# Two wide row loads put at passes 10 and 13, and the sums of three weight tiles kept from the first mixing for the second

## The chip, the cores and the metric

The kernel runs on one core of one Trainium2 chip. The metric is the device time of one execution in microseconds (us); the median of several runs counts. A profiled execution has a time of its own and a span, which is the time from its first instruction to its last. Matrix products run on TensorE (PE in the profile's rows; PEld is its loading of weights), elementwise work on VectorE (DVE) and ScalarE (ACT), and DMAs are issued by SyncE (SP) and GpSimd (POOL).

## The reference

Four layers on an x of 2048 rows by 512 columns in float32. Layers 0 and 2 are a Fourier mixing, layers 1 and 3 a gated feed-forward network:

```python
def _A_ref(x, dft_seq_re, dft_seq_im, dft_hid_re, dft_hid_im):
    a = jnp.einsum("bsd,ed->bse", x, dft_hid_re)
    b = jnp.einsum("bsd,ed->bse", x, dft_hid_im)
    return jnp.einsum("ts,bse->bte", dft_seq_re, a) - jnp.einsum("ts,bse->bte", dft_seq_im, b)

def _B_ref(x, w_gate, w_up, w_down):          # 512 -> 1792 -> 512
    return (_gelu(x @ w_gate) * (x @ w_up)) @ w_down

x = A_x
x = x + _A_ref(_layernorm(x), ...)
x = x + _B_ref(_layernorm(x), ...)
x = x + _A_ref(_layernorm(x), ...)
x = x + _B_ref(_layernorm(x), ...)
```

## The kernel before

Every float32 product is made of three: each operand is split into a high part of reduced precision and the rest, and high by high, high by rest and rest by high are summed (`mm3`, lines 211 to 215). A split (`split`, lines 154 to 158) is a copy on ScalarE (L156) and a subtraction on VectorE (L158). Tiles of 128 x 512 live in 98 slots of on-chip memory, which are taken and given back in order; the two wide tiles, `xwide` and `wide`, hold 512 rows of x each and are lent out as eight more slots while they are not used for x.

**The products take seven multiplications in place of eight** (Strassen's way, in a form with few additions). So operands are cut in four quarters A11, A12, A21, A22, and sums S1 to S4 of them are needed. In a mixing (layers 0 and 2) the sequence matrix is worked through in four blocks of 512 output rows. For each block the stages are A11, A12, S2 (which holds the products with S2, S1 and S3), S4, and the products with the hidden matrix. With `FORE` at 4, all four blocks run A11 first, then all four run A12, then block 0 goes on with S2. For each k of 8 in S2, `make_s2` takes the loaded tiles a21, a22 and a11 and makes three sums of them on VectorE (one addition, L196, and two subtractions, L189); `make_s4` makes the fourth from a12. The matrix is the same in layers 0 and 2. For two tiles of the last block the sums are made ahead, in layer 1 (`summed_ahead`), stored in `wss`, and loaded by the second mixing.

**The feed-forward layers** run in two windows of 1024 rows (w = 0, 1). A window has 14 passes (`up`) over the gate and up matrices, with products of the down matrix beside them (`beside`), and then the remaining products of the down matrix (the `late` list). With all seven pairs of the hidden blocks done in the seven-product form (`SEVEN` is 7: layer 1 in both windows and layer 3 in its first), the window's result is added to two wide tiles of x (`turned_into`) which `load_turned(0)` and `load_turned(1)` fill with four DMAs of 256 KB each (L1508, through `moved`), and `rows_done` stores them (L1515). `beside` calls `load_turned(0)` in the fourteenth pass; another call follows behind the passes, and `load_turned(1)` comes a third of the way through `late`.

**Other work in the queues.** In layer 1's second window row tiles of x are loaded (L241) for the statistics that the next mixing's normalisation needs (`terms_ahead`, `norm_terms`, L614 to L619 on ScalarE), and `seed` (L207) copies a bank of sums on ScalarE so that TensorE can go on adding to it.

**What sets the order.** Each engine and each DMA queue runs its own instructions in a fixed order. That order is made when the kernel is built: a planner goes through the program with its own durations, and an engine that is free takes the next instruction whose inputs it thinks ready, so a load can be pulled far ahead of its place in the program. `tc.issue_after(i)` is how the program holds this back: an instruction traced under it stands behind i in its engine's order, without a wait of its own. `stream["last"]` is the latest load of the stream of matrix tiles (`load_next`, L333), which runs a bounded number of items ahead of the products.

Of the kernel before, what the change touches and what calls it, by code (L numbers as in the profile page):

```python
# [9 lines left out]
F32 = mybir.dt.float32  # L10
# [4 lines left out]
P = 128  # L15
# [5 lines left out]
NB = S // TB  # L21
# [8 lines left out]
LAG = 6  # L30
NEAR = 3, 2, 6
EARLY = 2
EARLY_FROM, EARLY_EACH = 8,2
PACE = 9
SKEW = 2, 1
# [10 lines left out]
LATER = 3  # L46
LET = 5
SUMMED = 2
DOWN_RUNS = ((0,0,0,0),(4,4,4,0),(4,4,4,0),2)


@with_exitstack
def fnet_geglu(ctx: ExitStack, tc: tile.TileContext, x_in, ws, wh, wgu, wdn, wdc, whc, out):
# [32 lines left out]
    nc = tc.nc  # L86
# [80 lines left out]
    def split_slot(src):  # L167
        hi, lo = sb.get(F32R), sb.get(F32R)
        split(src, hi, lo)
        return hi, lo  # L170
# [129 lines left out]
    whs = {(m, c): dram.tile([P, 1024], F32, name=f"wh{m}_{c}") for m in range(2) for c in range(ND)}  # L300
    wds = {f: dram.tile([P, 1024], F32, name=f"wd{f}") for f in range(NF)}
    wdd = {k: dram.tile([P, 7 * 512], F32, name=f"wc{k}") for k in range(NF // 2)}
    wss = {k: [dram.tile([P, 512], F32, name=f"ws{k}_{i}") for i in range(4)] for k in range(SUMMED)}
    whd = {k: dram.tile([P, 7 * 512], F32, name=f"wq{k}") for k in range(ND)}
    pieces = (("A11", "A12"), ("S2", "S3"), ("S1", "A22"), ("S4",))

# [54 lines left out]
    def plain(v):  # L361
        p = split_slot(v)
        sb.put(v)
        return p
# [20 lines left out]
            return split_slot(v)  # L385
        return run

    def make_s2(k):
        def run(a21, a22, *a11):
            a11 = a11[0] if a11 else held.pop(k)  # L390
            plus(a22, a21, a22)
            minus(a21, a11, a21)
            minus(a11, a22, a11)
            s1s[k], s2s[k], s3s[k] = a22, a11, a21
            return split_slot(a11)
        return run

# [3 lines left out]
    def make_s3(k):  # L401
        return lambda: plain(s3s.pop(k))

    def make_s4(k):
        def run(a12):
            v = s2s.pop(k)
            minus(a12, a12, v)
            sb.put(v)
            return plain(a12)
        return run  # L410

# [74 lines left out]
    NP = NF // 2  # L486
# [16 lines left out]
    def mix_items(layer):  # L503
        def raw(make, *tiles):
            items.append((F32, tiles, make, None))

        for b, what in plan(layer):
            tiles = [[ws[(b * 2 + m) * NS + k] for k in range(NS)] for m in range(2)]
            (a11, a12), (a21, a22) = ((r[:NK], r[NK:]) for r in tiles)
            hold = b >= FORE[layer]  # L510
            if what == "A11":
                for k in range(NK):
                    raw(as_is if bare(layer, b, what, k) else make_a11(k) if hold else plain, a11[k])
            elif what == "A12":
                for k in range(NK):
                    raw(plain, a12[k])
            elif what == "S2":
                for i, k in skewed(3):
                    if layer and b == NB - 1 and k < SUMMED:
                        raw(plain, wss[k][i])  # L520
                    elif i == 0:
                        raw(make_s2(k), a21[k], a22[k], *(() if hold else (a11[k],)))
                    else:
                        raw(make_s1(k) if i == 1 else make_s3(k))
            elif what == "S4":
                for i, k in skewed(2):
                    if layer and b == NB - 1 and k < SUMMED and i == 0:
                        raw(plain, wss[k][3])
                    elif i == 0:
                        raw(make_s4(k), a12[k])  # L530
                    else:
                        raw(plain, a22[k])
            elif b in PAIRED.get(layer, ()):
                items.extend(pair_items(what))
            else:
                for m, c in what:
                    if layer == 0 and b == 0:
                        items.append((F32, (wh[m * ND + c],), make_hid_first(m, c), (m, c)))
                    else:
                        items.append((F32R, halves(whs[m, c]), make_hid(m, c), (m, c)))  # L540
# [666 lines left out]
    def summed_ahead(k):  # L1207
        t = []

        def load():  # L1210
            for m, i in ((1, k), (1, NK + k), (0, k), (0, NK + k)):
                t.append(sb.get())
                with tc.issue_after(stream["last"].ins):
                    nc.sync.dma_start(t[-1], ws[((NB - 1) * 2 + m) * NS + i])

        def sums():
            before, in_order[0] = in_order[0], True
            a21, a22, a11, a12 = t
            plus(a22, a21, a22)
            minus(a21, a11, a21)  # L1220
            minus(a11, a22, a11)
            minus(a12, a12, a11)
            for to, v in zip(wss[k], (a11, a22, a21, a12)):
                nc.gpsimd.dma_start(to, v)
            sb.put(*t)
            in_order[0] = before

        return load, sums
# [29 lines left out]
    def geglu(w, layer):  # L1258
# [77 lines left out]
        def beside_next(n, down):  # L1336
            beside_mix(n)
            next(down, None)

        def up(n):  # L1340
            if n + 3 in making:
                making[n + 3][0]()
            if n + 2 in making:
                queue.extend(making[n + 2][1])
            if n > 2 or w:
                for _ in range(DOWN_RUNS[3]):
                    run = down_making.pop(0) if down_making else None
                    if run:
                        run()
            product(n, chain[n], "S2", "T2", False, True)  # L1350
            u[n] = copied(chain[n])
            down = beside(n)
            beside_next(n, down)
            side[n] = ps8.get()
            product(n, side[n], "S1", "T1", True, True)
            w4[n] = copied(side[n])
            beside_next(n, down)
            first(n + 1)
            beside_mix(n)
            product(n, chain[n], "S3", "T3", False, True)  # L1360
            v = w4.pop(n)
            plus(v, v, chain[n])
            finished(n, 1, 1, v)
            sb.put(v)
            beside_next(n, down)
            product(n, side[n], "S4", "B22", False, True)
            v = u.pop(n)
            plus(v, v, side[n])
            ps8.put(side.pop(n))
            finished(n, 0, 1, v)  # L1370
            sb.put(v)
            beside_next(n, down)
            second(n + 1)
            if pairs == NP:
                for name, k in down_order(layer, w)[1][:max(0, n - EARLY_FROM) * EARLY_EACH]:
                    if k in h4:
                        prepared(name, k)
            product(n, chain[n], "A22", "T4", False, True)
            ps = chain.pop(n)
            if n % 2 == 0:  # L1380
                v = copied(ps)
                finished(n, 1, 0, v)
                sb.put(v)
            else:
                finished(n, 1, 0, ps)
            ps8.put(ps)
            beside_next(n, down)
            for _ in down:
                pass
# [111 lines left out]
        def outside(at, part):  # L1501
            return begun[part] if at == layer + 1 and pairs < NP else xs[at, w * 2 + part]

        def load_turned(part):
            assert part or not sb.out("x")
            pool = tpool if part else upool
            xturned[part] = pool.tile([P, NT * D], F32, name="wide" if part else "xwide")
            moved(xturned[part], outside(layer, part), lambda v, rows: nc.sync.dma_start(v, rows))  # L1508

        def turned_rows(part, c, src):  # L1510
            turned_into(xturned[part], c, src)
# [89 lines left out]
                slow.pop(0)()  # L1601
        if plain_down:
            load_rows(0)
        elif pairs == NP:
            load_turned(0)
        if w == 0:
            queue.extend([None] * 9 + others[len(ahead_of_all):ND] + ([] if ahead_of_all else [None] * 4) + others[ND:])
# [20 lines left out]
        else:  # L1628
# [3 lines left out]
            for i, (name, k) in enumerate(late):  # L1632
                if name == "S4" and pairs < NP:
                    break
                if pairs < NP and name == "S1" and k > 1:
                    prepared("S4", k - 2)
                for more in late[i:i + EARLY + 1]:
                    prepared(*more)
                for _ in down_product(name, k):
                    pass  # L1640
                if i == len(late) - HOLD:
                    late_end.append(newest["PE"])
                if not before_mix or i % 3 == 0:
                    step()
                if before_mix and i == len(late) // 2:
                    stream["more"] = MORE
                if i == len(late) // 3:
                    load_turned(1)
                    if w == 0:
                        queue[:2 * len(ahead)] = [run for pair in zip(ahead, queue) for run in pair] + queue[len(ahead):2 * len(ahead)]  # L1650
                while w == 0 and len(queue) > 2 * (len(late) - 1 - i):
                    step()
# [123 lines left out]
```

## Time and profile before

| | |
|---|---|
| three runs | 1596.91, 1599.49, 1601.11 us; median 1599.49 |
| profiled execution | 1599.44 us, span 1597.5 us |
| DMA | 431.74 MB, mean 270 GB/s |
| HBM | 344.46 MB read, 85.72 MB written |
| granted TensorE clock | full throughout |

A row of a group or of a time-ordered view gives a start and a length in us (or count, busy time and mean), the engine, the line of the kernel, the operation, what it writes and reads (buffer numbers left out), and in square brackets how long the engine idled before it and who ended the wait. "SPq" is the SP queue's issuing. Rows of a stretch give its two ends, its length, the busy time of each engine with its count of instructions, the granted clock, the DMA engines' busy share and GB/s; asked for one engine or line, they show that alone. Matmuls overlap, so a busy TensorE is best judged by the distance between starts.

### The profile page before, as it was taken

What the parts mean: (1) busy time and instruction counts of PE and PEld (TensorE: products, weight loads), DVE (VectorE), ACT (ScalarE), POOL (GpSimd) and SP (SyncE); (2) the same over time, 40 slices, a digit from 0 to 9 for tenths busy, and PEclk for the clock granted to TensorE, in tenths of its full rate; (3) what the DMA queues carried; (4) which work ended last, traced back from release to release, by engine and by line L of the source; (5) the groups of instructions that cost most, each with busy time, mean ns of one, the idle gap of its engine ahead of it and who ended that gap; (6) DMA issues with size and microseconds to landing.
All of it is one profiled execution on the core that took longest, in us unless ns stands there. A gap on an engine that the chain in (4) does not pass through costs nothing.

```text
span 1597.5 us, 22834 instructions
## 1 busy us (share of the span) xinstructions
PE 1589.7 (100%) x6984; PEld 1310.1 (82%) x6984; DVE 1176.7 (74%) x2042; ACT 890.4 (56%) x1731; POOL 293.6 (18%) x493
## 2 busy tenths in 40 slices
PE   9999999999999999999999999999999999999999
PEld 6888888888888888788888888888888888888887
DVE  8997878888689794665879867777895557844573
ACT  8955465754767653566648545556553565333460
POOL 4112121351457101330031000001301000000000
PEclk9999999999999999999999999999999999999999
DMA  9878888996998999997895876878978968895445
GB/s 363 290 264 295 305 307 280 356 309 202 316 363 315 278 323 294 350 361 238 290 299 187 272 242 213 271 247 249 257 257 277 273 213 256 296 295 173 132 145 158
DMA packets 249433, 431.74 MB, mean 270 GB/s; under 512 B 29344, under 2 KB 74656, under 8 KB 248288
## 3 DMA queue, kind: packets, MB, share of 16 engines
q1 hardware_dynamic: 220464, 340.36, 67.3%
q0 software_dynamic: 26160, 87.84, 15.3%
q10 hardware_dynamic: 2688, 2.10, 0.5%
q8 instruction: 55, 0.90, 0.2%
q14 instruction: 66, 0.54, 0.1%
HBM read 344.46 MB, written 85.72 MB: 269 GB/s over the span
## 4 chain that ended last, share of the span: by engine, by line
PE 90%; DMA 3%; issue 3%; ACT 2%; DVE 1%; POOL 1%; SPq 0%; POOLq 0%; ACTq 0%; DVEq 0%
PE p L214 30%; PE p L213 30%; PE p L215 30%; DMA s<-t 1%; ACT s L156 1%; DVE s L158 1%; PE p L999 1%; DMA xwide<-x 1%; DMA s<-x 1%; DMA s<-ws 0%; POOL rstd L617 0%; PE p L1682 0%; ACT s L200 0%; ACT p L207 0%; DVE s L189 0%
## 5 line engine op out<-in xcount | busy, mean ns | idle before, releaser
L214 PE MATMUL p<-s,s 128*128 128x512 f32 x2312 | 897.7, 389 | 0.8 <-DVE s L158 0.8
L215 PE MATMUL p<-s,s 128*128 128x512 f32 x2312 | 892.3, 389 | 0.0
L213 PE MATMUL p<-s,s 128*128 128x512 f32 x2312 | 858.2, 389 | 1.6 <-ACT p L207 1.5
L156 ACT ACTIVATE s<-s 128x512 fp32r<-128x512 f32 (+1 forms) x859 | 483.1, 608 | 266.1 <-DVE s L189 66.9
L158 DVE TENSOR_TENSOR s<-s,s 128x512 fp32r<-128x512 f32 (+1 forms) x859 | 540.1, 663 | 111.9 <-ACT s L156 94.8
L213 PEld LDWEIGHTS p<-s,s 128*128 128x128 f32 x2312 | 433.8, 188 | 93.6 <-ACT p L207 2.6
L214 PEld LDWEIGHTS p<-s,s 128*128 128x128 f32 x2312 | 433.9, 188 | 92.1 <-DVE s L158 2.3
L215 PEld LDWEIGHTS p<-s,s 128*128 128x128 f32 x2312 | 433.9, 188 | 90.4
L193 DVE TENSOR_TENSOR s<-s,p 128x512 f32<-128x512 f32 x199 | 134.7, 683 | 163.2 <-PE p L215 136.6
L189 DVE TENSOR_TENSOR s<-s,s 128x512 f32<-128x512 f32 (+1 forms) x415 | 245.1, 612 | 4.7 <-DMA s<-ws 2.2
L200 ACT ACTIVATE s<-p 128x512 f32<-128x512 f32 x232 | 134.4, 593 | 112.6 <-PE p L215 108.5
L1253 ACT ACTIVATE s<-s 128x512 f32<-128x512 f32 x84 | 52.8, 628 | 46.4 <-DVE s L193 46.1
L617 POOL TENSOR_SCALAR rstd<-rstd 128x1 f32<-128x1 f32 x40 | 23.2, 580 | 239.3 <-ACT s L616 231.5
L1253 ACT ACTIVATE s<-p 128x512 f32<-128x512 f32 x28 | 16.7, 596 | 83.2 <-PE p L215 83.2
L319 POOL DMA_DIRECT2D wb<-s x84 | 46.2, 552 | 91.2 <-ACT s L156 68.9
L640 ACT ACTIVATE s<-s,shift,rstd 128x512 f32<-128x512 f32 x59 | 47.6, 812 | 16.9 <-DVE shift L607 9.7
L1269 DVE TENSOR_TENSOR s<-s,p 128x512 f32<-128x512 f32 x56 | 38.3, 684 | 24.7 <-PE p L215 24.7
L158 DVE TENSOR_TENSOR s<-xwide,s 128x512 fp32r<-128x512 f32 (+1 forms) x49 | 32.8, 679 | 25.2 <-ACT s L156 25.2
L196 DVE TENSOR_TENSOR s<-s,s 128x512 f32<-128x512 f32 (+1 forms) x73 | 44.2, 613 | 6.8 <-DMA s<-ws 3.8
L207 ACT ACTIVATE p<-p 128x512 f32<-128x512 f32 x56 | 32.6, 584 | 24.2 <-PE p L215 23.9
L729 DVE STREAM_TRANSPOSE wide<-s 128x512 f32<-128x512 f32 x31 | 21.9, 708 | 25.8 <-ACT s L640 21.8
L1190 POOL DMA_DIRECT2D wc<-s x42 | 30.6, 730 | 54.0 <-ACT s L156 36.3
(104 smaller groups left out, 621.8 us busy)
## 6 DMA issues: line engine op xcount, KB each, us to landing
s<-ws SPq DMA_DIRECT2D x406, 256.0 KB, 5.0
s<-wb SPq DMA_DIRECT2D x294, 256.0 KB, 5.2
s<-wc SPq DMA_DIRECT2D x182, 256.0 KB, 4.6
wb<-s POOLq DMA_DIRECT2D x98, 256.0 KB, 5.2
s<-wh SPq DMA_DIRECT2D x84, 256.0 KB, 5.3
s<-x SPq DMA_DIRECT2D x53, 256.0 KB, 5.3
wc<-s POOLq DMA_DIRECT2D x49, 256.0 KB, 5.3
xwide<-ws SPq DMA_DIRECT2D x36, 256.0 KB, 4.9
```

The source lines that it names most:

```text
L156: newest["ACT"] = nc.scalar.activation(hi, src, AF.Copy)
L158: newest["DVE"] = nc.vector.tensor_tensor(lo, src, f32(hi), op=ALU.subtract)
L189: nc.vector.tensor_tensor(out, a, b, op=ALU.subtract)
L193: bank_read["DVE"] = nc.vector.tensor_tensor(out, a, b, op=ALU.add)
L196: nc.vector.tensor_tensor(out, a, b, op=ALU.add)
L200: bank_read["ACT"] = nc.scalar.activation(v, src, AF.Copy)
L213: nc.tensor.matmul(ps, ah, bh, start=start, stop=False, skip_group_check=True)
L214: nc.tensor.matmul(ps, ah, bl, start=False, stop=False, skip_group_check=True)
L215: newest["PE"] = nc.tensor.matmul(ps, al, bh, start=False, stop=stop, skip_group_check=True)
L319: nc.gpsimd.dma_start(a, f32(t))
L640: nc.scalar.activation(z, x, AF.Identity, bias=shift, scale=rstd)
L1253: nc.scalar.activation(t, g, AF.Gelu_apprx_tanh)
```

## The change

Two things are changed. In layer 1's second window `load_turned(0)` is called in the tenth pass and `load_turned(1)` in the thirteenth; in that window their DMAs are put behind the latest load of the matrix stream. The calls behind the passes and in `late` are left out where the tile is there already; the call in `beside` stays as it was. And in the first mixing's block 0 the four sums of tiles k = 0, 1, 2 are stored to memory by GpSimd's queue as they are made; the second mixing's block 0 loads them in place of the tiles and the sums.

```diff
+TURNED = 9, 12
+KEPT = ((0, 0), (0, 1), (0, 2))
...
-    wss = {k: [dram.tile([P, 512], F32, name=f"ws{k}_{i}") for i in range(4)] for k in range(SUMMED)}
+    wss = {
+        (b, k): [dram.tile([P, 512], F32, name=f"ws{b}_{k}_{i}") for i in range(4)]
+        for b, k in [*KEPT, *((NB - 1, k) for k in range(SUMMED))]
+    }
...
+    def sums_kept(layer, at, sums):
+        if layer == 0 and at in KEPT:
+            for i, v in sums.items():
+                nc.gpsimd.dma_start(wss[at][i], v)
+
-    def make_s2(k):
+    def make_s2(layer, b, k):
         def run(a21, a22, *a11):
             a11 = a11[0] if a11 else held.pop(k)
             plus(a22, a21, a22)
             minus(a21, a11, a21)
             minus(a11, a22, a11)
             s1s[k], s2s[k], s3s[k] = a22, a11, a21
+            sums_kept(layer, (b, k), {0: a11, 1: a22, 2: a21})
             return split_slot(a11)
...
-    def make_s4(k):
+    def make_s4(layer, b, k):
         def run(a12):
             v = s2s.pop(k)
             minus(a12, a12, v)
             sb.put(v)
+            sums_kept(layer, (b, k), {3: a12})
             return plain(a12)
...
-                    if layer and b == NB - 1 and k < SUMMED:
-                        raw(plain, wss[k][i])
+                    if layer and (b, k) in wss:
+                        raw(plain, wss[b, k][i])
...
-                    if layer and b == NB - 1 and k < SUMMED and i == 0:
-                        raw(plain, wss[k][3])
+                    if layer and (b, k) in wss and i == 0:
+                        raw(plain, wss[b, k][3])
...
             beside_next(n, down)
+            if (layer, w) == (1, 1) and n in TURNED:
+                load_turned(TURNED.index(n))
             side[n] = ps8.get()
...
-            moved(xturned[part], outside(layer, part), lambda v, rows: nc.sync.dma_start(v, rows))
+            with tc.issue_after(stream["last"].ins) if (layer, w) == (1, 1) else ExitStack():
+                moved(xturned[part], outside(layer, part), lambda v, rows: nc.sync.dma_start(v, rows))
...
-        elif pairs == NP:
+        elif pairs == NP and not xturned:
             load_turned(0)
...
                 if i == len(late) // 3:
-                    load_turned(1)
+                    if 1 not in xturned:
+                        load_turned(1)
```

More of the change, by code (lines that the diff above doesn't have):

```diff
@@ L518, in mix_items @@
                 for i, k in skewed(3):
-                    if layer and b == NB - 1 and k < SUMMED:
-                        raw(plain, wss[k][i])
+                    if layer and (b, k) in wss:
+                        raw(plain, wss[b, k][i])
                     elif i == 0:
-                        raw(make_s2(k), a21[k], a22[k], *(() if hold else (a11[k],)))
+                        raw(make_s2(layer, b, k), a21[k], a22[k], *(() if hold else (a11[k],)))
                     else:
@@ L526, in mix_items @@
                 for i, k in skewed(2):
-                    if layer and b == NB - 1 and k < SUMMED and i == 0:
-                        raw(plain, wss[k][3])
+                    if layer and (b, k) in wss and i == 0:
+                        raw(plain, wss[b, k][3])
                     elif i == 0:
-                        raw(make_s4(k), a12[k])
+                        raw(make_s4(layer, b, k), a12[k])
                     else:
@@ L1222, in sums @@
             minus(a12, a12, a11)
-            for to, v in zip(wss[k], (a11, a22, a21, a12)):
+            for to, v in zip(wss[NB - 1, k], (a11, a22, a21, a12)):
                 nc.gpsimd.dma_start(to, v)
```

## The prediction

> **What bounds the kernel now.** I read the page first (engine totals and the chain), then the list of who waited for whom on TensorE, then the time-ordered views around each stall, and last the stretches into which the change moves work.
>
> ```profile
> span 1597.5 us, 22834 instructions
> PE 1589.7 (100%) x6984; PEld 1310.1 (82%) x6984; DVE 1176.7 (74%) x2042; ACT 890.4 (56%) x1731; POOL 293.6 (18%) x493
> ...
> PE p L213 <- ACT p L207: 1.5, 2, 1.3
> PE p L1682 <- POOL ident masks.py:199: 1.4, 1, 1.4
> PE p L214 <- DVE s L158: 0.8, 1, 0.8
> ```
>
> The first two lines are the page, the last three are all the waits of TensorE: 3.7 us in the whole span, of which 1.4 us lie in the warm-up. TensorE sets the time, the change touches no matmul (x6984 stays), so it can only win back stalls or add new ones. Two stalls matter, and each part of the change stands beside one of them. The first, in order of time on TensorE, on ScalarE and on the SP queue:
>
> ```profile
> 642.73 0.39 PE L214 MATMUL p<-s,s 128*128 128x512 f32 x1
> 642.95 0.39 PE L215 MATMUL p<-s,s 128*128 128x512 f32 x1
> 644.67 0.50 PE L213 MATMUL p<-s,s 128*128 128x512 f32 x1 [1.33 <-ACT p L207]
> 645.01 0.40 PE L214 MATMUL p<-s,s 128*128 128x512 f32 x1
> ...
> 643.41 0.63 ACT L614 ACTIVATE s<-s 128x512 f32<-128x512 f32 x1 [3.63 <-DMA s<-x]
> ...
> 644.04 0.58 ACT L207 ACTIVATE p<-p 128x512 f32<-128x512 f32 x1
> ...
> 615.99 2.78 SPq L1508 DMA_DIRECT2D wide<-x  x4
> 618.88 3.08 SPq L1243 DMA_DIRECT2D s<-wb  x2
> 622.13 4.01 SPq L1508 DMA_DIRECT2D xwide<-x  x4
> ...
> 635.76 3.29 SPq L1508 DMA_DIRECT2D xwide<-x  x4
> ...
> 634.60 8.79 DMA s<-x
> ...
> s<-x SPq DMA_DIRECT2D x53, 256.0 KB, 5.3
> ```
>
> Matmuls start 0.22 to 0.23 us apart; from 642.95 to 644.67 it is 1.72, so 1.49 is lost, and the next start comes 0.34 later, another 0.11: 1.60 us. TensorE waits for the seed of a bank (L207). That seed is ready to run but stands on ScalarE behind L614, the statistics of a row tile for the next mixing, which idled 3.63 us for its load. That load took 8.79 us (last but one line, from the chain) against a median of 5.3 (last line, the page). Eight DMAs of wide tiles stand just ahead of it on SP, and four more just behind it: all twelve belong to this very window (layer 1, second half), though the program asks for them 120 us later or more. They were pulled ahead as soon as the tiles were free.
>
> The second stall:
>
> ```profile
> 889.64 1.07 PE L213 MATMUL p<-s,s 128*128 128x512 f32 x4
> 891.55 0.50 PE L214 MATMUL p<-s,s 128*128 128x512 f32 x1 [0.84 <-DVE s L158]
> 891.88 0.39 PE L215 MATMUL p<-s,s 128*128 128x512 f32 x1
> ...
> 891.12 1.07 POOL L291 DMA_DIRECT2D m_sum<-s  x2 [6.12 <-ACT s L200]
> ...
> 872.00:891.50 19.50, 19.50 (x34) 1.00 0.87 292
> 872.00:891.50 19.50, 6.43 (x11) 1.00 0.87 292
> 872.00:891.50 19.50, 3.44 (x5) 1.00 0.87 292
> ...
> 876.95 4.91 DMA s<-ws
> ...
> 884.18 0.69 DVE L196 TENSOR_TENSOR s<-wide,s 128x512 f32<-128x512 f32 x1
> ```
>
> Four starts from 889.64 would put the next at 890.55; it comes at 891.55, and the one behind 0.33 later: 1.00 + 0.10 = 1.10 us. The store of m_sum at 891.12 carries out the last sums of the fourth block's A12, so this is the seam to S2 of block 0 in the second mixing. The three stretches are VectorE whole, its L189 alone (subtractions) and its L196 alone (additions): VectorE works without a gap for 19.5 us before the stall, and 16 of its 34 instructions are the sums of S2. The split (L158) that TensorE waits for queues among them.
>
> **Part 1: wide tiles of layer 1.** The issuing line's own rows are
>
> ```profile
> L1508 SPq DMA_DIRECT2D xwide<-x x28: 303/492/1813, 408.4 to 1421.8; - x28
> L1508 SPq DMA_DIRECT2D wide<-x x16: 303/487/2025, 518.7 to 1407.5; - x16
> ```
>
> 28 against 16: `load_turned(0)` runs twice in the three windows with all seven pairs, once in the fourteenth pass (`beside`) and once behind the passes. The new condition `not xturned` drops the second one, 4 DMAs of 256 KB each in layer 1's first window and in layer 3's first. Beside the stall of 1.3 us the list of TensorE's waits leaves 0.2 us for L207 and nothing else, so I put this at nothing. In layer 1's second window the diff adds a load in passes 10 and 13, but `beside` asks again in pass 14 without a check: twelve DMAs before, twelve after, only later and behind the weight stream on SP. So 2.78 + 4.01 = 6.79 us of SP issue ahead of the 634.60 load go, and 3 MB beside it. Only 1.60 us are needed for the stall to go; the load's excess over the median alone, 8.79 − 5.3 = 3.5, is more. What comes late next on ScalarE is the matmul result itself, which costs nothing. I take −1.60; bounds −1.60 and 0.
>
> What the moved loads can cost:
>
> ```profile
> 705.00:725.00 20.00, 20.00 (x90) 16.57 (x89) 15.05 (x24) 9.38 (x21) 6.93 (x10) 1.00 1.01 367
> 725.00:745.00 20.00, 20.00 (x90) 16.55 (x89) 11.62 (x18) 9.01 (x15) 0.00 (x0) 1.00 0.55 177
> 745.00:765.00 20.00, 20.00 (x90) 16.55 (x89) 12.61 (x23) 17.56 (x33) 0.00 (x0) 1.00 0.88 291
> ...
> 704.79 0.45 SPq L241 DMA_DIRECT2D s<-x  x1
> ...
> 714.39 0.63 ACT L614 ACTIVATE s<-s 128x512 f32<-128x512 f32 x1 [0.76 <-PE p L215]
> ...
> 775.26 0.65 DVE L196 TENSOR_TENSOR xwide<-xwide,s 128x512 f32<-128x512 f32 x1
> ```
>
> A pass is 48 matmuls, 10.9 us; counted from the window's first matmul at about 601, passes 10, 13 and 14 begin near 702, 735 and 745. The last two numbers of the stretches are DMA share and GB/s. The bursts of passes 13 and 14 meet 0.55 and 0.88; that of pass 10 meets a full stretch, and the row load of 704.79 stands behind it. At 5.3 us it lands at 710.1 and is used at 714.39: 4.3 us of cover, against the 3.5 us that such bursts cost the load at 634.60. So it holds, barely. The tile loaded last (pass 14) is first written at 775.26, 30 us after its pass begins, where the longest burst above needed 4.01 us to issue and 8.79 bounds a landing. Value 0, bounds 0 and +1.60 for a burst that catches a row load as the old ones did.
>
> **Part 2: stored sums.** In the second mixing, block 0, three tiles lose two subtractions and one addition in S2 and one subtraction in S4: 12 instructions of VectorE. By the rows above one costs 6.43/11 = 0.58 to 3.44/5 = 0.69; nine of them, 5.3 to 6.2 us, go from the full stretch or its edge. The loads stay as many. VectorE cannot use all of it: the load of 876.95 landed at 881.86, and the addition of 884.18 is the next large step that needs such tiles, so 2.3 us is what is sure. That is over 1.10. Value −1.10, bounds −1.10 and 0.
>
> In the first mixing, block 0, twelve stores of 256 KB are added on GpSimd's queue (3.15 MB):
>
> ```profile
> 85.45 0.69 DVE L196 TENSOR_TENSOR s<-s,s 128x512 f32<-128x512 f32 x1
> ...
> 88.51 1.07 POOL L291 DMA_DIRECT2D m_sum<-s  x2 [9.96 <-ACT s L200]
> 96.49 0.54 POOL L291 DMA_DIRECT2D m_sum<-s  x1 [6.91 <-ACT s L200]
> ...
> 85.00:106.00 21.00, 21.00 (x94) 17.41 (x93) 21.00 (x35) 14.46 (x28) 2.16 (x4) 1.00 0.87 304
> ...
> 126.38 1.28 DVE L193 TENSOR_TENSOR s<-s,p 128x512 f32<-128x512 f32 x2 [5.63 <-ACT s L200]
> ...
> wb<-s POOLq DMA_DIRECT2D x98, 256.0 KB, 5.2
> ```
>
> GpSimd is busy 2.16 of 21 us there; twelve issues at 0.54 are 6.5 us that nobody waits for. The sums begin at 85.45, and TensorE reaches S2 near 96.5 (the fourth block's sums leave then): 11.0 us of lead. DMA moves 304 GB/s at share 0.87, so 349 when full: 45 spare over 21 us are 0.95 MB, and the other 2.2 MB push loads back by 6.3 us. Lead covers it. Value 0, bounds 0 and the price of the slower rival.
>
> A store also is issued while VectorE is never free (21.00 of 21). The two at 88.51 took 1.07 us together, 0.54 each, as the one at 96.49 did; no sign of a lock. The Trainium skill, SBUF — State Buffer, "Who interferes with whom", says that VectorE and GpSimd share one pair of ports as an exclusive lock, so that one blocks the other for a whole instruction; by that rule VectorE would lose up to 12 × 0.54 = 6.5 us here, still under the lead, and the rows speak against even that.
>
> **The sum.** 1599.44 (the profiled execution; span 1597.5 and 1.9 around it) − 1.60 − 1.10 = 1596.7. The median of the three runs is 1599.49, so it carries over; those runs reach from 1596.91 to 1601.11, and about 0.3% (4.8 us) is what a measurement can tell from no change. The two stalls together are 2.7 us, so a gain over 0.3% would need nearly all of TensorE's other waits and luck as well.
>
> **The rivals.** *One stall stays or comes back.* Either the burst of pass 10 (or 13, 14) catches a row load and ScalarE stops in front of a seed again, +1.60, or the split at 891 is limited by arrival of the loads and stays, +1.10. For it: 4.3 us of cover against 3.5, and a DMA share of 1.01. Against: two of three bursts meet free room. 1596.7 + 1.60 = 1598.3, or 1597.8.
>
> *The stores push the first mixing (slower).* If the stores go ahead of all loads, 3.15 MB at 349 GB/s hold them for 9.0 us; a slot whose tile is being stored can be refilled only when the store has landed, 5.2 us more on the in-order SP queue: 14.2 against 11.0 of lead. VectorE has no gap until the 5.63 us before 126.38 to catch up. TensorE then stalls 14.2 − 11.0 = 3.2 us at S2 of block 0, or, where nothing of the lead is rebuilt by block 0's end, 14.2 − 5.6 = 8.6: 1599.9 to 1605.3, middle 1602.6. It turns the sign from a slip of 11.0 + 2.7 = 13.7 us. For it: VectorE and DMA are full there. Against: the share falls to about half behind 106, and stores and loads share the engines.
>
> The Trainium skill, TensorE: Matmul & The Clock Gate, Part 1, adds that TensorE falls to half its clock after about 3.4 us without work; with that, a stall of 8.6 us would cost some 2 us more (an estimate from that page). No stall behind the warm-up is that long here, so no row shows it.
>
> *Nothing changes.* Both stalls have another cause than I read: 1599.4. Against it stand the rows of both.
>
> **How the numbers follow.** Forecast 0.50; one stall left 0.22; slower rival 0.16; nothing 0.08; a further gain, where the smaller stalls go as well, 0.04. The range runs from 1594.6 (forecast less the 2.1 us that runs scatter downward from about their middle) to 1602.6 (the slower rival's middle). Faster by over 0.3% (below 1594.7): 0.05. Slower by over 0.3% (above 1604.3): 0.10, the upper end of the slower rival and a new order of a queue that I do not see. Within: 0.85.
>
> **What would show it.** Right: line 1508's issues fall to 20 for xwide and stay 16 for wide; VectorE 2030 instructions, GpSimd 505, TensorE 6984; HBM read less by 2.1 MB (8 loads), written more by 3.1. No wait for L207 near 643, and none for a split near 890. Wrong: ScalarE at L614 waiting for a row load between 700 and 770 with a TensorE gap behind it; a gap of TensorE between 85 and 130; a TensorE wait total of more than 3.7 us.

## The result and the profile after

The changed kernel is slower: 1600.93 us median of 22 runs against 1598.47 of 22 runs of the kernel before, ratio 1.0016 with a 95% interval of 1.0010 to 1.0022, or 2.5 us. That lies between the 1594.6 and 1602.6 of the prediction and is a difference of less than 0.3%, but it went the other way: 1596.7 was forecast, a gain of 2.7.

The page of the changed kernel has the counts that the prediction named:

```profile
span 1600.7 us, 22828 instructions
PE 1591.7 (99%) x6984; PEld 1309.5 (82%) x6984; DVE 1169.0 (73%) x2030; ACT 891.2 (56%) x1731; POOL 295.1 (18%) x505
HBM read 342.36 MB, written 88.87 MB: 269 GB/s over the span
```

Its list of TensorE's waits answers to the three rows of before. Neither of the two old stalls is in it; other waits are:

```profile
PE p L215 <- DMA s<-wb: 1.3, 1, 1.3
PE p L215 <- ACT s L202: 1.3, 2, 0.7
PE p L217 <- DVE s L160: 0.3, 1, 0.3
```

(Lines 215 to 217 are the matmuls that were 213 to 215; L202 copies a bank out, L160 is the second half of a split, L1523 the wide loads, L1255 the weight pieces wb, L243 the row loads, L626 begins the statistics of a row tile as L614 did before, L652 is the normalisation.) On TensorE's own time view:

```profile
717.08 0.39 PE L217 MATMUL p<-s,s 128*128 128x512 f32 x1
718.21 0.50 PE L215 MATMUL p<-s,s 128*128 128x512 f32 x1 [0.74 <-ACT s L202]
...
721.30 0.39 PE L217 MATMUL p<-s,s 128*128 128x512 f32 x1
722.97 0.50 PE L215 MATMUL p<-s,s 128*128 128x512 f32 x1 [1.28 <-DMA s<-wb]
...
756.65 0.39 PE L215 MATMUL p<-s,s 128*128 128x512 f32 x1
757.56 0.50 PE L215 MATMUL p<-s,s 128*128 128x512 f32 x1 [0.52 <-ACT s L202]
```

With 0.23 us from start to start, and about 0.11 more at the matmul behind each stall, these cost 1.01, 1.55 and 0.79 us: 3.35 together. The span is 3.2 us longer in all: the two old stalls are won, and beside the three new ones there are 0.8 us at 852, 0.4 near 1172, some smaller ones, and 0.6 in the start. What lies ahead of the three stalls is seen on the SP queue, and in three rows of the chain of waits that ends at 722.97:

```profile
698.80 0.58 SPq L1523 DMA_DIRECT2D xwide<-x  x1
...
702.28 2.57 SPq L1523 DMA_DIRECT2D xwide<-x  x3
704.95 2.14 SPq L1255 DMA_DIRECT2D s<-wb  x3
...
707.58 0.32 SPq L243 DMA_DIRECT2D s<-x  x1
...
736.39 2.01 SPq L1523 DMA_DIRECT2D wide<-x  x4
738.45 4.77 SPq L1523 DMA_DIRECT2D xwide<-x  x4
```

```profile
698.80 7.90 DMA xwide<-x
...
706.72 8.32 DMA s<-wb
...
715.10 7.82 DMA s<-wb
```

The burst of pass 10 stands at 699 to 705, and pieces of the gate and up weights behind it take 8.32 and 7.82 us to land, where the page before had a median of 5.2 for such loads (s<-wb; 4.9 over the whole kernel after). TensorE runs out of them at 721. The three rows of the chain follow on each other. In every trace kept here, SP issues no DMA before the one eight places ahead of it on its queue has landed: the wide load of 698.80 lands at 706.70, and the piece eight places behind it is issued at 706.72. So loads that land late also hold back the issue of those behind them, and the burst is still felt by a piece issued ten microseconds after it. What sets the eight, the chip or the way the program is built, isn't shown.

The stall at 717 is that of a row load. It is the one that the prediction had at 704.79; it stands behind the burst, is issued at 707.58 and takes 8.1 us to land (5.1 before). ScalarE waits for it, and the bank copy that TensorE needs stands behind its statistics:

```profile
715.87 0.63 ACT L626 ACTIVATE s<-s 128x512 f32<-128x512 f32 x1 [3.20 <-DMA s<-x]
...
717.58 0.58 ACT L202 ACTIVATE s<-p 128x512 f32<-128x512 f32 x1
```

The eight loads of passes 13 and 14 stand together at 736 to 743; ScalarE then waits 4.99 us for a row load, and a bank copy stands behind that one too:

```profile
754.28 1.52 ACT L652 ACTIVATE s<-s,shift,rstd 128x512 f32<-128x512 f32 x2 [4.99 <-DMA s<-x]
```

The stretches show the same: the loads left a place that now has room, and filled those that they came to (the last two numbers are DMA share and GB/s). The first row is of the kernel before, the others are of the changed one; the other rows of before stand in the prediction.

```profile
625.00:645.00 20.00, 18.67 (x82) 15.14 (x82) 11.69 (x22) 9.80 (x20) 4.94 (x7) 1.00 1.13 257
...
625.00:645.00 20.00, 20.00 (x89) 16.54 (x89) 11.68 (x21) 10.57 (x22) 5.66 (x9) 1.00 0.77 253
...
705.00:725.00 20.00, 17.98 (x79) 14.23 (x78) 14.29 (x24) 8.22 (x19) 4.55 (x9) 1.00 1.08 338
725.00:745.00 20.00, 20.00 (x90) 16.58 (x89) 10.91 (x18) 9.22 (x16) 0.62 (x2) 1.00 0.99 292
745.00:765.00 20.00, 19.48 (x87) 15.79 (x86) 8.55 (x16) 12.61 (x26) 0.00 (x0) 1.00 1.01 296
```

### The profile page after: what moved, and what is told of

Same layout as the page of the kernel before. It is cut to its first block, busy times and chain, and to the rows that moved or that the text cites. A ratio compares the mean times of both kernels' runs of the same rounds, so it can differ in the third digit from the quotient of the medians.

```text
span 1600.7 us, 22828 instructions
## 1 busy us (share of the span) xinstructions
PE 1591.7 (99%) x6984; PEld 1309.5 (82%) x6984; DVE 1169.0 (73%) x2030; ACT 891.2 (56%) x1731; POOL 295.1 (18%) x505
## 4 chain that ended last, share of the span: by engine, by line
PE 93%; DMA 3%; issue 2%; ACT 1%; POOL 1%; DVE 0%; SPq 0%; ACTq 0%; POOLq 0%
PE p L215 31%; PE p L217 31%; PE p L216 31%; DMA s<-wb 2%; DMA xwide<-x 0%; PE p L1011 0%; DMA s<-x 0%; POOL rstd L629 0%; ACT s L158 0%; ACT s L652 0%; DMA s<-ws 0%; POOL s L755 0%; DVE s L160 0%; POOL wb L324 0%; ACT p L209 0%
## 5 line engine op out<-in xcount | busy, mean ns | idle before, releaser
L160 DVE TENSOR_TENSOR s<-s,s 128x512 fp32r<-128x512 f32 (+1 forms) x855 | 536.5, 662 | 116.8 <-ACT s L158 99.9
L202 ACT ACTIVATE s<-p 128x512 f32<-128x512 f32 x232 | 134.5, 593 | 109.2 <-PE p L217 105.9
L652 ACT ACTIVATE s<-s,shift,rstd 128x512 f32<-128x512 f32 x59 | 47.6, 811 | 20.6 <-DVE shift L619 11.5
L160 DVE TENSOR_TENSOR s<-xwide,s 128x512 fp32r<-128x512 f32 (+1 forms) x52 | 34.9, 679 | 32.0 <-ACT s L158 31.8
L158 ACT ACTIVATE s<-xwide 128x512 fp32r<-128x512 f32 (+1 forms) x52 | 31.6, 621 | 24.1 <-DVE xwide L195 18.1
```

Of the source, the lines that this page charges most:

```text
L158: newest["ACT"] = nc.scalar.activation(hi, src, AF.Copy)
L160: newest["DVE"] = nc.vector.tensor_tensor(lo, src, f32(hi), op=ALU.subtract)
L202: bank_read["ACT"] = nc.scalar.activation(v, src, AF.Copy)
L652: nc.scalar.activation(z, x, AF.Identity, bias=shift, scale=rstd)
```

## The experiments

Two theories stood against each other. **Burst**: the wide loads meet a full stretch of DMA and delay loads that somebody waits for; the stores cost nothing. **Replan**: the twelve stores shift the planner's clock, and a new order of the queues makes new stalls wherever it likes. TensorE's instructions stand in the same order in the kernel before, the change and its parts, as far as operations and tiles go; those of VectorE, ScalarE and the queues mostly don't.

| kernel | median us | kernel before, run beside it | ratio, 95% interval | lost by TensorE at 700 to 770, us |
|---|---|---|---|---|
| the change | 1600.93 | 1598.47 | 1.0016 [1.0010, 1.0022] | 3.4 |
| sums alone | 1598.34 | 1598.81 | 0.9997 [0.9987, 1.0007] | 0 |
| wide loads alone | 1600.97 | 1598.81 | 1.0017 [1.0008, 1.0026] | 2.0 |
| held, pass 14 and late | 1601.57 | 1598.81 | 1.0017 [1.0008, 1.0027] | 0; 5.0 at 772 |
| no reload | 1600.12 | 1598.81 | 1.0012 [1.0004, 1.0021] | 1.0 |
| passes 12 and 13 | 1598.34 | 1598.71 | 0.9997 [0.9988, 1.0006] | 0 |
| both in pass 10 | 1606.07 | 1598.71 | 1.0044 [1.0032, 1.0057] | 8.2 |
| drop alone | 1598.24 | 1598.71 | 0.9997 [0.9988, 1.0006] | 0 |
| a quarter in pass 10 | 1598.20 | 1598.44 | 1.0005 [0.9996, 1.0013] | 0 |
| passes 12 and 13, no sums | 1599.18 | 1598.44 | 1.0003 [0.9994, 1.0012] | 0 |
| passes 12 and 13, five sums | 1598.77 | 1598.44 | 1.0004 [0.9995, 1.0013] | 0 |

The ratio is an estimate with its interval and needn't be that of the two medians. The last column is worked out from the starts of the matmuls in one profiled execution, as above.

**Sums alone.** The wide loads are put back as they were:

```diff
-            if (layer, w) == (1, 1) and n in TURNED:
-                load_turned(TURNED.index(n))
...
-            with tc.issue_after(stream["last"].ins) if (layer, w) == (1, 1) else ExitStack():
-                moved(...)
+            moved(...)
-        elif pairs == NP and not xturned:
+        elif pairs == NP:
```

> The change with its wide loads put back as they were; only the stored sums of three tiles remain. Burst theory (the four wide loads of pass 10 meet a full DMA stretch and delay weight pieces that TensorE waits for; the stores cost nothing): no stall at 717, 721 or 756 us, the stall at 643 stays (1.6 us), the one at 890 is gone, so 1.1 us faster than before. Replan theory (the twelve stores shift the planner's clock and the new order makes new stalls): new stalls of together 2 us or more after 640 us, equal to before or slower.

No stall between 700 and 760 and no loss: the replan theory, as far as it goes by the stores, falls here. But the gain of 1.1 us isn't seen either (0.5 us, give or take 1.6). The stall at 890 is gone, and TensorE stops for 0.5 us at 899 and for 1.75 at 907, in the same stage S2. Its time view and VectorE's:

```profile
906.31 0.84 PE L215 MATMUL p<-s,s 128*128 128x512 f32 x3
908.63 0.50 PE L216 MATMUL p<-s,s 128*128 128x512 f32 x1 [1.48 <-DVE s L160]
```

```profile
896.34 0.69 DVE L191 TENSOR_TENSOR s<-s,s 128x512 f32<-128x512 f32 x1 [2.02 <-DMA s<-ws]
...
898.25 0.69 DVE L198 TENSOR_TENSOR s<-xwide,s 128x512 f32<-128x512 f32 x1 [1.23 <-DMA s<-ws]
```

VectorE, without a gap before, now idles for loads of the tiles whose sums it still has to make. In this execution the time that the stored sums freed is waited away, and the stall falls on later tiles.

**Wide loads alone.** `KEPT` is empty.

```diff
-KEPT = ((0, 0), (0, 1), (0, 2))
+KEPT = ()
```

> The change without its stored sums; only the wide loads move. Burst theory: the stall at 643 is gone (-1.6), stalls near 717, 721 and 757 together 3.4 us come, the stall at 890 stays: 1.8 us slower than before. Replan theory: without the stores no stall between 700 and 760, so 1.6 us faster than before.

The whole loss comes with the wide loads alone (their move changes the order of VectorE and ScalarE too; passes 12 and 13 below keep it). The stalls stand at 717, 721 and 755, shorter in this execution (0.3, 0.8 and 0.8 us). The stall at 890 wasn't there, though nothing was done against it; 0.7 us were lost at 850 instead. So that stall comes and goes.

**Held, but at the old places.** No loads in passes 10 and 13; each tile is loaded once, `xwide` by the call in pass 14, `wide` a third of the way through the late list.

```diff
-            if (layer, w) == (1, 1) and n in TURNED:
-                load_turned(TURNED.index(n))
```

> The whole change, but no wide load in passes 10 and 13: the tiles are asked for in pass 14 and a third of the way through the late list, each once, still behind the matrix stream on SP. Burst theory: no stall at 643, 717, 721 or 757; 3.4 us less than the change, 0.9 us less than before. If passes 14 and the late list have no room either: a stall of 1 to 3 us between 745 and 800 in its place. Replan theory: stalls between 700 and 760 stay, time as the change.

Clean up to 770, then the longest stall so far. First the SP queue, then ScalarE, TensorE and a stretch behind the stall:

```profile
760.09 2.01 SPq L1521 DMA_DIRECT2D wide<-x  x4
...
765.20 0.43 SPq L243 DMA_DIRECT2D s<-x  x1
```

```profile
771.92 0.81 ACT L652 ACTIVATE s<-s,shift,rstd 128x512 f32<-128x512 f32 x1 [6.74 <-DMA s<-x]
```

```profile
772.14 0.39 PE L217 MATMUL p<-s,s 128*128 128x512 f32 x1
775.65 0.50 PE L215 MATMUL p<-s,s 128*128 128x512 f32 x1 [3.12 <-ACT s L202]
...
777.15 0.63 PE L216 MATMUL p<-s,s 128*128 128x512 f32 x1
```

```profile
776.00:780.00 4.00, 4.00 (x12) 3.13 (x11) 4.00 (x8) 4.00 (x9) 0.00 (x0) 0.57 1.00 368
```

This is the rival of the prediction, a burst that catches a row load, at another place: the wide loads of 760 stand before the row load of 765, ScalarE idles 6.74 us, and TensorE 3.12. It also costs clock: the stretch behind it has a granted clock of 0.57 on the mean, and matmuls start 0.43 us apart for some 3 us. The Trainium skill's page TensorE: Matmul & The Clock Gate, Part 1, says that an idle TensorE falls to half its clock until it has been busy for about 3.4 us. This trace agrees. But the page puts the idle that it takes at about 3.4 us as well, and here 3.12 us were enough.

**No reload.** The call in pass 14 is left out where the tile is there.

```diff
-                if k == pairs - 1:
+                if k == pairs - 1 and 0 not in xturned:
```

> The whole change, but the reload in pass 14 is left out, so eight wide loads in place of twelve: four in pass 10, four in pass 13. Burst theory: stalls at 717 and 721 stay (2.6 us), the one at 757 shrinks from 0.8 us to nothing as half of the burst before it goes; 0.8 us less than the change. If the stall at 757 stays, the pass 13 load alone is enough for it. Replan theory: no telling where, about as the change.

The stall at 757 is gone and one at 721 stays (0.8 us, with 0.2 at 717), smaller than the 2.6 us expected. The median is 0.8 us under the change's, but the intervals overlap.

**Passes 12 and 13.** As the last one, with the first load two passes later, so that the order of all engines but SP stays the same, row by row.

```diff
-TURNED = 9, 12
+TURNED = 11, 12
```

> The whole change, but the first load stands in pass 12 in place of 10 and the reload in pass 14 is left out: four loads in pass 12, four in pass 13, where the stretch before had a DMA share of 0.55. All engines but SP keep the order of the kernel that only leaves out the reload. Burst theory: no stall at 717 or 721, none at 757; 1 to 2.5 us less than that kernel, at or below before (-1 us). Rival, any load in the second half of this window costs, since a full stretch comes before and behind: a stall of 1 us or more between 735 and 775, time as the change.

Nothing is lost between 700 and 770, and the median falls by 1.8 us against the same loads in pass 10. The intervals, 0.9988 to 1.0006 and 1.0004 to 1.0021, barely touch. Only the SP queue differs: four wide loads stand later, and a few loads near them change places. The stretch from 725 to 745 is now full as well (DMA share 1.09, 298 GB/s), and TensorE doesn't stall: as far as these runs go, a full stretch costs only where one of the loads behind is needed soon.

**Both in pass 10.**

```diff
-            if (layer, w) == (1, 1) and n in TURNED:
-                load_turned(TURNED.index(n))
+            if (layer, w) == (1, 1) and n == TURNED[0]:
+                load_turned(0)
+                load_turned(1)
```

> The change with both tiles loaded in pass 10, eight loads in a row, and no reload in pass 14. Burst theory: the dose doubles, so the stalls at 717 and 721 grow from 1.1 to 2.6 us (two runs) to 3 to 6 us, and the median rises by 2 to 3 us over the kernel with one tile there. Rival, the time is lost elsewhere: stalls at 717 to 725 as before, time as that kernel.

TensorE's waits, and ScalarE's time view (L626 begins the statistics of a row tile):

```profile
PE p L215 <- ACT s L158: 6.4, 1, 6.4
```

```profile
724.13 0.63 ACT L626 ACTIVATE s<-s 128x512 f32<-128x512 f32 x1 [8.50 <-DMA s<-x]
```

Twice the burst gives one stall of 6.5 us and 1.7 more by the slower clock behind it, 8.2 in all, over the 3 to 6 that were expected. It is the same row load again, now the one that comes last. It is issued only at 714.60, 9.8 us later than in the kernel before, with eight slow loads ahead of it; in the prediction its cover was 4.3 us.

**Drop alone.** The kernel before with only the second, useless load of `xwide` left out.

```diff
-        elif pairs == NP:
+        elif pairs == NP and not xturned:
```

> The kernel before, with nothing changed but the condition that leaves out the second load of the wide tile behind the passes: 12 fewer DMAs of 256 KB, the order of all engines but SP as before. In layer 1's second window the four loads just behind the row load of 634.6 go, the eight ahead of it stay. If the crowd ahead makes the stall at 643: it stays at 0.5 to 1.6 us and the time is that of before. If the whole crowd makes it: it goes, up to 1.6 us faster.

No stall at 643 in this execution, 1.6 us lost at 882 to 891, and no difference in time. As the kernel before, unchanged, can do without the stall at 643 too (next run), this doesn't say which loads make it.

**The kernel before again.** Unchanged.

> The kernel before, unchanged, for a second look. If the stall of 1.6 us at 643 is what this order always gives, it is there again within 0.3 us; the kernel with only the stored sums, whose order is the same there, showed 0.4. If its length hangs on how the DMAs of one execution fall, it lies anywhere between 0 and 2 us, and my term for it was one draw, not a mean.

```profile
PE p L1682 <- POOL ident masks.py:199: 1.4, 1, 1.4
PE p L213 <- ACT p L207: 0.2, 1, 0.2
```

These are all its waits. Both stalls on which the prediction rests are missing, in a span of 1594.8 us. At 643 the same order lost 1.60, 0 and, with the sums alone (where all queues stand the same up to there but for the first mixing), 0.41 us.

**A quarter in pass 10.** Four issues in pass 10 as without the reload, but each of 64 KB; the other three quarters in pass 12.

```diff
+        def load_part(first):
+            if first:
+                xturned[0] = upool.tile([P, NT * D], F32, name="xwide")
+            cut = slice(0, 4) if first else slice(4, 16)
+            with tc.issue_after(stream["last"].ins):
+                moved(xturned[0], outside(layer, 0), lambda v, rows: nc.sync.dma_start(v[:, cut], rows[:, cut]))
```

> As the kernel that leaves out the reload (xwide in pass 10, wide in pass 13), but in pass 10 only a quarter of each of the four pieces is loaded, 64 KB in place of 256, the other three quarters in pass 12; the same four issues in the same places of the SP queue in pass 10. If the bytes on the DMA engines delay the weight pieces: the stalls at 717 to 723 go or fall under 0.5 us, and the median falls 1 to 2 us, to that of the kernel with both loads moved back (1598.3). If holding the in-order SP queue delays them: stalls and median as with the whole load (1 to 2.6 us, 1600.1).

The stretch of the kernel without the reload, and that of this one:

```profile
705.00:725.00 20.00, 19.43 (x85) 15.53 (x84) 15.06 (x25) 8.00 (x18) 5.17 (x10) 1.00 1.08 337
...
705.00:725.00 20.00, 20.00 (x90) 16.57 (x89) 15.50 (x25) 9.00 (x20) 5.21 (x10) 1.00 1.03 353
```

TensorE works through this stretch, and the row load behind the burst takes 4.8 us to land, where it took 8.1 without the reload. So, in the one execution of each that was profiled, it is what the loads carry that delays the others, not that four of them stand in the queue. The time says the same less firmly: 1.0005 against 1.0012, with intervals that overlap.

**Passes 12 and 13 without the sums, and with five.** `KEPT` is empty in the one and has k = 0 to 4 in the other.

```diff
-KEPT = ((0, 0), (0, 1), (0, 2))
+KEPT = ()
+KEPT = ((0, 0), (0, 1), (0, 2), (0, 3), (0, 4))
```

> The loads in passes 12 and 13 alone, without the stored sums. If part 2 is worth its 1.1 us once the wide loads are out of the way: 1.1 us slower than with the sums (1599.4), with a stall at 890 of 1 us. If the stored sums only hand the stall on to the next tiles of S2 (stall at 905 in place of 890): as with the sums within 0.5 us, and no stall between 895 and 910.

> As the kernel with the loads in passes 12 and 13, but with the sums of five tiles stored in place of three. If the stall at 905 is that of the first tiles whose sums are still made there: it moves behind 910 or goes, up to 1 us faster (1597.4). If the load stream is what is late, it stays near 905 with 0.5 to 1.8 us. If twenty stores in place of twelve hurt the first mixing, a stall between 85 and 130 that no other kernel has.

Without the sums the stall is at 889 (1.2 us), with three at 905 (1.0), with five at neither, but 1.3 us are then lost at 847. The times of the three (0.9997, 1.0003 and 1.0004, each ±0.0009) can't be told apart: with three against none the sums gain 1.0 us, give or take 2.0 (the two intervals in quadrature). With five, the slower rival appears in the first mixing, in TensorE's view and in the chain of waits:

```profile
110.59 0.50 PE L216 MATMUL p<-s,s 128*128 128x512 f32 x1 [0.92 <-DVE s L160]
```

```profile
97.17 11.97 DMA s<-ws
```

A load of a tile takes 11.97 us to land among twenty stores, and VectorE and then TensorE wait for it: 1.2 us lost.

**The change again.** Unchanged.

> The changed kernel again, for a second look. Burst theory: stalls at the same two places, 717 and 721, and at 757, together between 1 and 5 us, since the order is the same and only the DMAs' timing differs; none at 643. Rival, the stalls of the first look were chance: two of the three places clean.

```profile
PE p L215 <- DMA s<-wb: 1.6, 1, 1.6
PE p L215 <- ACT s L202: 0.6, 2, 0.4
```

(TensorE's waits for those two.) The stalls are back at 717, 721 and 757: 0.7, 1.9 and 0.4 us, 3.0 together. This execution also lost 0.7 us at 105, in the first mixing, with twelve stores.

## Why the prediction was wrong, point by point

**What bounds the kernel** was right: TensorE's count is unchanged and only stalls move the time.

**The two gains were one draw.** 1.60 and 1.10 us were taken from a single execution. Three executions of the order before have 1.60, 0.41 and 0 us at 643, 0.7 on the mean; at 890, two executions of the kernel before have 1.10 and 0. The span without both is seen in the second of these, 1594.8. Counting against the profiled execution's own time made the gain look like all of 2.7 us, while by these means (0.7 and 0.55) about 1.2 us were there to be won.

**What the moved loads cost was put at nothing, and that is the step that failed.** The prediction weighed the row load of 704.79, 4.3 us of cover against 3.5 us of longer landing: "So it holds, barely." It didn't hold. That sum left out that the burst also goes ahead of this load on the SP queue. In the change it is issued 2.8 us later and lands 3.0 us slower, 5.8 together, and ScalarE comes there 1 us sooner, with the stall at 643 gone. That makes the stall at 717, by the very sign that the prediction named as wrong: ScalarE waiting for a row load, with a TensorE gap behind it. The pieces of the gate and up weights, which stand on the same queue behind the burst, were not weighed at all; TensorE waits for them without another engine between, and that is the stall at 721. The bursts of passes 13 and 14, which were to meet free room, caught a row load too (757). The first rival put a price on one caught row load, 1.60; measured are 3.4 and 3.0 us at the three places, 3.2 on the mean. Less the 0.7 that the old stall cost on the mean, that is 2.5 us, like the measured difference. That they agree to the tenth is luck: two executions of each kernel were profiled, and they differ at other places too, by 1.1 us at 890 alone.

**The time of a burst was not worked out.** It was taken from what the old bursts did to one load, 3.5 us. The DMA view of the kernel before over 600 to 660 us, 40 slices of 1.5 us, has in its first row the busy share in tenths and in its second GB/s:

```profile
DMA  8999999999999999999999999999999999999999
GB/s 302 284 367 335 318 329 320 391 386 317 356 356 318 179 197 202 194 249 175 198 208 206 251 389 406 390 183 170 224 318 383 403 392 385 354 366 280 279 395 412
```

Behind the wide issues of 616 to 626 and of 636 to 639 the engines are as busy as ever and move 170 to 251 GB/s, in place of mostly 320 to 412. A wide tile is read in pieces of 128 numbers, 512 bytes: by the two pages, the change has eight of these loads fewer and 4096 packets fewer from 512 B up to 2 KB. So 1 MB takes some 5 us of all engines (an estimate: 1.05 MB at 200 GB/s), where the 349 GB/s that the prediction used for the stores would give 3.

Two smaller slips of that part changed nothing. By the prediction's own figures (601 and 10.9 us a pass) passes 10, 13 and 14 begin at 699, 732 and 743, not at 702, 735 and 745. And 8.79 us doesn't bound a landing: the loads of `xwide` at 600 to 660 in the kernel before have a median of 9.6.

**The reload of pass 14** was seen in the diff, and put at nothing like the others: it costs the 0.4 to 0.8 us at 757, as the execution without it shows none.

**VectorE's relief** came as worked out, and its limit too, but in the wrong place: I named the load of 881.86 as the next late thing and reckoned 2.3 us as sure. The loads stayed late for the tiles behind it, and the stall moved to 905 or 907 in three kernels with three stored sums (sums alone, passes 12 and 13, a quarter in pass 10). The kernels with these sums that lose time at 700 to 780, the change among them, show none at 890 to 910; whether that lost time lets the loads catch up was not tested. Measured alone, the sums gained 0.5 us, give or take 1.6, which is not told from nothing.

**The slower rival** (stores push the first mixing) is real with twenty stores and shows 0.7 us in one of the eight executions profiled with twelve; it isn't what made the change slower, since the sums alone were not. Its chance of 0.16 was the wrong place for the weight of a slower time: the rival of one caught load, extended to several loads, should have had it.

Left open is what makes the stall at 852, 0.8 us in one execution of the change and 0.4 in the other; it was there without the sums too (0.7 at 850), and not in the execution without the reload. No run was made for it.

## What to carry to other kernels

When a load is moved, list everyone behind it on its queue and on the full DMA engines, not only who caught it before: a load that costs nothing in a full stretch at one place isn't free at another. For each of them add both delays, that it is issued later and that it lands slower, and hold the sum against its cover. A stall of one execution is a draw: profile it twice before it is entered as a gain. Where the first tile of a stage is late, relieving it can hand the wait to the next tile unless the loads come earlier too.

## What the runs showed of the hardware

Fully busy DMA engines moved about 200 GB/s (170 to 251) behind the wide loads with their pieces of 512 bytes, and mostly 320 to 412 otherwise. SP had no more than eight DMAs under way: in all fourteen traces none is issued before the one eight places ahead of it has landed. TensorE lost half its clock after an idle of 3.12 us (granted clock 0.57 behind it, matmuls 0.43 us apart), and not after those of 1.3 and 1.6 us, where only the next start came 0.11 us late. The length of a stall in one fixed order changed from one execution to the next by up to 1.6 us.
